# Clustered attention, soft MoE and a PReLU layer on one core: q's rounded part through PSUM, norm steps with a PSUM operand, a new order of attention's steps

## Chip, cores and metric

The kernel runs on one core of one Trainium2 chip. The metric is the device time of one execution in microseconds (us); lower is better. The time before is 498.64 us, the median of three runs (496.78 to 499.43).

## What is computed

Three layers follow one another. The attention has 2 x 8 = 16 heads of 768 tokens and 64 dimensions. Each token of q and k is assigned to one of 16 centroids of its head, and a query sees only keys of its own cluster:

```python
q_n = q / (np.linalg.norm(q, axis=-1, keepdims=True) + 1e-06)
k_n = k / (np.linalg.norm(k, axis=-1, keepdims=True) + 1e-06)
q_assign = np.argmax(np.einsum('bhsd,hcd->bhsc', q_n, c_n), axis=-1)
k_assign = np.argmax(np.einsum('bhsd,hcd->bhsc', k_n, c_n), axis=-1)
mask = q_assign[:, :, :, None] == k_assign[:, :, None, :]
scores = np.where(mask, scale * np.matmul(q, k.transpose(0, 1, 3, 2)), -1e9)
attn = np.exp(scores - np.max(scores, axis=-1, keepdims=True))
attn = attn / (np.sum(attn, axis=-1, keepdims=True) + 1e-09)
x = np.matmul(attn, v)
```

The result, 1536 tokens of 512, goes through a soft mixture of 8 experts (x @ phi, two softmaxes, w1, relu, w2), and then through x @ w_in, a PReLU with a slope per column, and @ w_out. All of it is float32.

## The kernel before

The 16 heads are worked on in 8 pairs. A head has six steps of 128 keys. In a step c of head h, `s2(h, c)` (L500) makes the scores of 128 keys against 768 queries in two halves of 384 columns: two matmuls for each half on TensorE (L514), and the exponential on ScalarE (L517) out of PSUM. `av` (L535) multiplies them by v (L542), and `acc` (L524) adds them up on GpSimd (L530). Some ten steps ahead, `s1` (L433) makes the scores of the later head once in lower precision (L448), so that VectorE can take each query's maximum (L455); `mrow` (L463) turns the maxima into a row (L484, L486) that `s2` uses as one more row of its operand. After a head, `sums` (L564) and `xnat` (L582) turn the sums and the output by TensorE (L571, L589); VectorE scales the output into x (L593, L597). After a pair, `xtr` (L604) turns x (L610), ScalarE copies it out (L614), and `logit` (L619) multiplies it by phi.

For float32 accuracy from TensorE's rounded float32 type, q and k are each split in a rounded part and the remainder. `put_high` (L418) rounds into the operands A and B (L420). `high` (L399) rounds a pair's whole q or k into a buffer `hi` in SBUF (L401), and `low` (L403) takes the remainder, in place: for q on VectorE, 768 columns at once (L407), for k on GpSimd, in two halves (L411). There is one `hi` for q and k together. `put_low` (L422) moves the parts to their lanes with four DMAs on SP's queue (L100).

For the assignment, `asg_norm` squares and sums q and k, `asg_root` (L274) takes the root by a start value and three Newton steps on VectorE, with its working values in a PSUM bank that it holds, and `asg_rn` (L304) adds 1e-6 and inverts it. The squared norms `n2` lie in SBUF (the tile `n` in the trace), so the first step (L285) and the addition (L307) read and write SBUF alone. The pairs are taken in six groups; the first two use ScalarE's root instead. `asg_sims`, `asg_nat` and `asg_pick` then find the nearest centroid.

`misc` (L127) gives the two PSUM banks for all such small work in turn. While a step holds one (`asg_nat` until the third `asg_pick`, `asg_root`, `win_bits`), all others get the other bank.

The order of the work is fixed when the kernel is built. Each call is entered by `add(key, function, ..., need=...)` with a place on a line that counts steps (L731 to L848), the places come from `TABLE` (L25), and the calls are made in the order of their places, put off until their needs are met (L860 to L873). Each engine, and SP's queue of DMAs, works through its own instructions in that order. Weights are loaded on SP's queue between them (`load_w`, L185): 16 units of 1 MB in attention, the other 16 after it (L194).

```python
    def high(p, nm):
        hi[p, nm] = t = ear.tile([P, S], F32R, name="hi")
        act.activation(t, raws[p][nm], AF.Copy)
```

Of the kernel before, what the change touches and what calls it, by code (L numbers as in the profile page):

```python
# [7 lines left out]
F32 = mybir.dt.float32  # L8
F32R = mybir.dt.float32r
# [23 lines left out]
    t_lo=-6.45, i_hk=-27.3, i_ph=-28.95, i_lk=-25.2, i_rt=-19.95, i_et=-18.5, z_lo=-8.6, md=(0, 1),  # L33
    ld=(0, -0.2, 0, 0, 0.2), e_sum0=7.85, e_sum1=11.3, e_xnat=10.3, lead=4, s1=-0.85, av=1.55,
    sum0=7.7, sum1=9.6, xnat=11.35, xtr0=11.7, xtr1=11.7, logit=12.5, t_sum0=7.15, t_sum1=14,
    t_xnat=13.9, t_xtr0=14.7, t_xtr1=15.4, t_logit=21.1, u_sum0=7.65, u_sum1=7.85, u_xnat=10.7,
    mr0=-1.35, mr1=1.15, mr2=2.85, z_mr0=-4.5, z_mr1=2.85, z_mr2=3.05, ph0=-8.35, ph1=-7.7,
    oh=-7.55, lo=-2.95, v=-4.6, raw=-25.1, sims=-14.75, nat=-13.85, p0=-13.5, p1=-14.35, p2=-12.05,
# [1 line left out]
    y_p0=-14.95, y_p1=-13.2, y_p2=-14.65, y_oht=-11.3, y_hq=-6.75, y_hk=-1.3, y_lq=-5.5, y_lk=-4.1,  # L40
    y_rn=-3, rest=-11.1, x0=5.5, x2=56.3, d0=-3.35, d1=2.2, d2=3.4, d3=-2.5, nl0=-14.45, nl1=-9.2,
    nl2=-4.8, nl3=-2.8, no0=-7.7, no1=-3.5, no2=-1.7, no3=-0.5, nr0=0.5, nr1=1.7, nr2=2.95, nr3=3.7,
    nrn=5.35, dz=(-2.7, 8.2), do0=1.6, do1=2.5, do2=2.8, do3=4.45, do4=3.3, sp=15, lke=0,
    w7=(4, 10), wc=(6, 3, 8), pipe=6, ws=13, wk=(0, 0, 3, 6, 3, 3, 3, 0, 6, 0, 6, 3),
# [2 lines left out]
    w=(
        ('r', -4.7, -1.7),
        ('r', 3.9, 6.5),
        ('r', 16.1, 16.1),  # L50
        ('r', 25.1, 30.1),
        ('r', 38.5, 38.5),
        ('r', 46.5, 54.5),
        ('r', 52.7, 53.3),
        ('r', 60.1, 62.1),
        ('r', 75.5, 75.5),
        ('r', 78.3, 79.3),
        ('r', 83.24, 84.24),
        ('a', 90.3, 92.3),
        ('a', 90.4, 92.4),  # L60
        ('r', 91.3, 93.7),
        ('b', 94.4, 96),
        ('c', 100.8, 101.8),
# [1250 lines left out]
```

## Time and profile before

| what | us |
|---|---|
| median of the three runs | 498.64 |
| the three runs | 499.43, 496.78, 498.64 |
| span of the profiled execution, first to last instruction | 495.9 |
| its own whole time | not listed apart from the three above |
| TensorE busy in the span | 451.4 (91%) |
| VectorE busy | 342.1 (69%) |
| ScalarE busy | 294.5 (59%) |
| GpSimd busy | 217.1 (44%) |
| TensorE's mean granted clock, of full speed | 0.986 |

Attention takes the first 290 us or so, the experts go to about 340 us, and the last layer takes the rest. In the names of the engines, PE is TensorE, PEld its loading of weights, DVE VectorE, ACT ScalarE, POOL GpSimd, and SP the queue that issues the DMAs. A busy share is a mean over stages with different limits, so a stretch is read by what its engines waited for. "Busy" also holds the time in which an instruction had been started and was held up.

### The profile page before, as it was taken

The page shows a single profiled execution, that of the slowest core. Times are in us where ns is not written, and L with a number is a line of the kernel's source. Part 1 is how long each engine was busy: PE and PEld are TensorE (multiplying, and loading weights), DVE is VectorE, ACT ScalarE, POOL GpSimd, SP SyncE. Part 2 cuts the span into 40 slices and gives each one's busy share as a digit, 9 for nine tenths or more (in the row PEclk, how much of TensorE's full clock was granted, in tenths as well). Part 3 has the DMA queues.
Part 4 walks back from the last instruction along what each step waited for, and adds up shares of the span by engine and source line. Part 5 has one row for each costly group of instructions (what it writes and reads, how often), then busy time and mean ns, then how long its engine had stood idle before and what let it go on. Part 6 is the DMA issues. An engine that isn't in the chain of part 4 may idle for free.

```text
span 495.9 us, 7750 instructions
## 1 busy us (share of the span) xinstructions
PE 451.4 (91%) x2694; PEld 299.7 (60%) x2694; DVE 342.1 (69%) x576; ACT 294.5 (59%) x538; POOL 217.1 (44%) x243
## 2 busy tenths in 40 slices
PE   3669899899999998989999899979899999999996
PEld 0336455565565655656565455436678888888885
DVE  3886989978999788798863442135799996544442
ACT  4846586585866868667665421126989885433431
POOL 5104777588777887677878200002443331000000
PEclk9997889999999999999999999999999999999999
DMA  8596555685676767544647489999322001200003
GB/s 283 150 299 189 156 145 185 149 266 170 163 200 185 195 222 212 154 131 123 230 138 256 192 325 351 388 397 398 102 85 86 0 0 49 79 1 0 1 1 127
DMA packets 32410, 84.10 MB, mean 170 GB/s; under 512 B 4402, under 2 KB 4742, under 8 KB 32372
## 3 DMA queue, kind: packets, MB, share of 16 engines
q1 hardware_dynamic: 32372, 83.62, 51.7%
q8 instruction: 21, 0.34, 0.3%
q14 instruction: 17, 0.14, 0.1%
HBM read 66.36 MB, written 3.19 MB: 140 GB/s over the span
## 4 chain that ended last, share of the span: by engine, by line
PE 54%; DVE 5%; issue 3%; ACT 3%; DMA 3%; POOL 1%; SPq 0%; ACTq 0%; POOLq 0%; DVEq 0%
PE ob L1206 8%; PE ob L1204 8%; PE ob L1205 8%; PE s L514 7%; PE ot L542 7%; PE s L448 3%; DMA unit_wr<-in_w 3%; PE s L995 2%; PE hp L1168 2%; PE L L1017 1%; PE misc L571 1%; DVE cs L455 1%; PE s L558 1%; POOL unit_wr L1101 1%; DVE unit_wr L407 1%
## 5 line engine op out<-in xcount | busy, mean ns | idle before, releaser
L530 POOL TENSOR_TENSOR ss<-ss,pt 128x384 f32<-128x384 f32 x150 | 147.0, 1020 | 40.8 <-PE ot L542 40.8
L455 DVE TENSOR_REDUCE cs<-s 128x1 f32<-128x768 f32 x91 | 86.2, 948 | 31.2 <-PE s L448 31.2
L517 ACT ACTIVATE pt<-s 128x384 f32<-128x384 f32 x160 | 70.0, 488 | 53.7 <-PE s L514 50.7
L514 PE MATMUL s<-A,B 97*128 97x384 f32 (+1 forms) x384 | 95.3, 370 | 2.2 <-ACT pt L517 2.1
L514 PEld LDWEIGHTS s<-A,B 97*128 97x128 f32 (+1 forms) x384 | 64.0, 195 | 27.5 <-issue 14.8
L1204 PE MATMUL ob<-unit_wr,gh 128*128 128x512 f32 x192 | 75.2, 392 | 0.5 <-ACT gh L1192 0.5
L1205 PE MATMUL ob<-unit_wr,gh 128*128 128x512 f32 x192 | 75.0, 390 | 0.2 <-POOL unit_wr L1101 0.2
L1206 PE MATMUL ob<-unit_wr,gl 128*128 128x512 f32 x192 | 75.1, 391 | 0.0
L1101 POOL TENSOR_TENSOR unit_wr<-unit_wr 128x256 fp32r<-128x256 f32 x32 | 26.0, 834 | 106.9 <-ACT unit_wr L1094 104.3
L448 PE MATMUL s<-B,A 96*128 96x384 f32 x192 | 57.4, 385 | 6.0 <-DVE cs L455 5.0
L542 PE MATMUL ot<-pt,raw_v 128*64 128x384 f32 x320 | 62.1, 501 | 0.0
L1190 DVE SCALAR_TENSOR_TENSOR g<-hp,sal,hs 128x768 f32<-128x768 f32 (+1 forms) x34 | 32.7, 967 | 26.1 <-ACT hs L1188 26.0
L448 PEld LDWEIGHTS s<-B,A 96*128 96x128 f32 x192 | 34.2, 202 | 21.6 <-DVE cs L455 16.7
L1188 ACT ACTIVATE hs<-hp,sgn 128x768 f32<-128x768 f32 (+1 forms) x34 | 29.1, 863 | 27.0 <-PE hp L1168 26.7
L1194 DVE TENSOR_TENSOR gl<-g,gh 128x768 fp32r<-128x768 f32 (+1 forms) x34 | 31.1, 915 | 15.1 <-ACT gh L1192 14.9
L1206 PEld LDWEIGHTS ob<-unit_wr,gl 128*128 128x128 f32 x192 | 36.0, 188 | 8.1 <-DVE gl L1194 0.3
L1205 PEld LDWEIGHTS ob<-unit_wr,gh 128*128 128x128 f32 x192 | 36.1, 188 | 7.5 <-POOL unit_wr L1101 1.1
L1204 PEld LDWEIGHTS ob<-unit_wr,gh 128*128 128x128 f32 x192 | 36.0, 188 | 7.0 <-ACT gh L1192 0.7
L1192 ACT ACTIVATE gh<-g 128x768 fp32r<-128x768 f32 (+1 forms) x34 | 27.4, 807 | 18.3 <-DVE g L1190 18.2
L542 PEld LDWEIGHTS ot<-pt,raw_v 128*64 128x64 f32 x320 | 20.3, 137 | 27.2 <-issue 26.4
L411 POOL TENSOR_TENSOR unit_wr<-unit_wr,hi 128x384 fp32r<-128x384 f32 x16 | 15.7, 1003 | 30.1 <-ACT n L281 14.4
L684 POOL TENSOR_TENSOR unit_wr<-unit_wr 128x256 uint32<-128x256 uint32 x26 | 19.2, 761 | 16.1 <-ACT ss L517 16.1
(184 smaller groups left out, 641.3 us busy)
## 6 DMA issues: line engine op xcount, KB each, us to landing
unit_wr<-in_w SPq DMA_DIRECT2D x16, 1024.0 KB
unit_wr<-in_w SPq DMA_DIRECT2D x18, 512.0 KB
unit_wr<-in_w_in SPq DMA_DIRECT2D x16, 512.0 KB
unit_wr<-in_w_out SPq DMA_DIRECT2D x7, 1024.0 KB
unit_wr<-in_qn SPq DMA_DIRECT2D x8, 384.0 KB
unit_wr<-in_kn SPq DMA_DIRECT2D x8, 384.0 KB
unit_wr<-in_qT SPq DMA_DIRECT2D x8, 384.0 KB
unit_wr<-in_kT SPq DMA_DIRECT2D x8, 384.0 KB
```

The costliest lines, as they stand in the source:

```text
L448: pe.matmul(ps[hf], a[:96, c * P:c * P + P], b[:96, hf * 384:hf * 384 + 384], start=True, stop=True,)
L455: dve.tensor_reduce(m, t, axis=AX.XY, op=ALU.max, negate=True)
L514: pe.matmul(ps[:, :384], b[:, c * P:c * P + P], a[:, hs], start=(i == 0), stop=(i == 1))
L517: act.activation(e[:, hs], ps[:, :384], AF.Exp, scale=0.125)
L530: (pool if h < T["sp"] else dve).tensor_tensor(ss[h][:, hs], ss[h][:, hs], sme[h, c][:, hs], op=ALU.add)
L542: pe.matmul(ot[h][hf * 64:hf * 64 + 64, :], v[:, c, par * 64:par * 64 + 64], e[:, hf * 384:hf * 384 + 384], start=(c == 0), stop=(c == 5),)
L1101: pool.tensor_tensor(wlo(i)[:, c], top[:, c], wh(i)[:, c].bitcast(F32), op=ALU.subtract)
L1190: dve.scalar_tensor_tensor(g, hv, sal[:, f:f + 1], hs, op0=ALU.mult, op1=ALU.max)
L1194: dve.tensor_tensor(gl, g, gh.bitcast(F32), op=ALU.subtract)
L1204: pe.matmul(ob[t], gh[:, c], wh(f), start=(f == 0), stop=False)
L1205: pe.matmul(ob[t], gh[:, c], wlo(f), start=False, stop=False)
L1206: pe.matmul(ob[t], gl[:, c], wh(f), start=False, stop=(f == 15))
```

## The change

Seven of the eight pairs (all but the first, which is made ahead of the attention) have q split in halves of 384 columns. ScalarE writes the rounded half into a `misc` bank of PSUM, and VectorE subtracts it from q into a buffer of its own, `lowq`. Each half's subtraction is entered right behind its rounding. k goes on through `hi`, and GpSimd takes its remainder. In the Newton root, the first step and the last write to PSUM or read from it, with one small copy added, and the addition of 1e-6 reads PSUM; for the first two groups (the root on ScalarE) it stays as it was. The places in `TABLE` are all set anew; two lines of them stand below for the many. A scratch space for DMAs that GpSimd would issue is cut to 1024.

```diff
-    oht=-9.55, hq=-6.05, hk=-1.95, lq=-7.3, lk=-5.1, y_v=-6.1, y_sims=-22.7, y_nat=-14.5,
+    nat=-13.65, p0=-13.5, p1=-13.7, p2=-11.45, oht=-9.65, hq0=-6.1, hq1=-3.7, hk=-4.55,
+    lq0=-8.9, lq1=-4.9, lk=-3.75, y_v=-8.7, y_sims=-23.9, y_nat=-18.15, y_p0=-20.3, y_p1=-14,
...
         if i == 0:
 
-            dve.tensor_scalar(x, x, 1e-30, None, op0=ALU.max)
             w = misc(hold=True)
...
-            nwt[g] = y, t
+            nwt[g] = y, t, z
+            dve.tensor_scalar(z, x, 1e-30, None, op0=ALU.max)
+            dve.tensor_copy(x, z)
             dve.tensor_scalar(
-                z.bitcast(U32), x.bitcast(U32), 1, None, op0=ALU.logical_shift_right
+                z.bitcast(U32), z.bitcast(U32), 1, None, op0=ALU.logical_shift_right
             )
...
         if i == 3:
-            dve.tensor_tensor(x, y, x, op=ALU.mult)
+            dve.tensor_tensor(z, y, x, op=ALU.mult)
+            dve.tensor_scalar(x, z, 1e-6, None, op0=ALU.add)
 
     def asg_rn(g):
         n = len(BATCH[g])
         x = n2[g][:, :n, :]
-        dve.tensor_scalar(x, x, 1e-6, None, op0=ALU.add)
+        if g < 2:
+            dve.tensor_scalar(x, x, 1e-6, None, op0=ALU.add)
...
-    hi = {}
-
-    def high(p, nm):
+    hi, lows = {}, {}
+
+    def high(p, nm, hf=None):
+        if hf is not None:
+            hi[p, nm, hf] = ps = misc(F32R)[:, :384]
+            act.activation(ps, raws[p][nm][:, hf * 384:hf * 384 + 384], AF.Copy)
+            return
...
-    def low(p, nm):
+    def low(p, nm, hf=None):
 
         t = raws[p][nm]
-        if nm == "qT" or T["lke"]:
+        if hf is not None:
+            if hf == 0:
+                lows[p] = cor.tile([P, S], F32R, name="lowq")
+            n = slice(hf * 384, hf * 384 + 384)
+            dve.tensor_tensor(
+                lows[p][:, n], t[:, n], hi.pop((p, nm, hf)).bitcast(F32), op=ALU.subtract
+            )
+            return
+        if nm == "qT":
             dve.tensor_tensor(t.bitcast(F32R), t, hi[p, nm].bitcast(F32), op=ALU.subtract)
             return
...
-        move(a2[:64, :], raws[h // 2]["qT"][lanes(h), :])
+        move(a2[:64, :], lows.get(h // 2, raws[h // 2]["qT"])[lanes(h), :])
...
-            add(s0 + T[z + "hq"] - LEAD, high, p, "qT", need=[("raw", p)], tag=("hq", p))
             add(s0 + T[z + "hk"] - LEAD, high, p, "kT", need=[("raw", p)], tag=("hk", p))
-            add(s0 + T[z + "lq"], low, p, "qT", need=[("hq", p), ("si", p), ("ph0", 2 * p), ("ph0", 2 * p + 1)], tag=("lq", p))
+            for i in range(2):
+                add(s0 + T[z + f"hq{i}"], high, p, "qT", i, need=[("raw", p)], tag=("hq", p, i))
+                add(s0 + T[z + f"lq{i}"], low, p, "qT", i, need=[("hq", p, i)] + ([("lq", p, 0)] if i else [("lo", 2 * p - 1)]), tag=("lq", p, i))
...
-    nc = bacc.Bacc("TRN2", target_bir_lowering=False, num_devices=1)
+    nc = bacc.Bacc(
+        "TRN2", target_bir_lowering=False, num_devices=1, dynamic_dma_scratch_size=1024
+    )
```

What the new places do is seen at the end of an odd head, here head 3, where pair 1 is finished and pair 3's q is split. VectorE's order there, before: `xnat` (L593, L597), the subtraction for q (L407), the maximum for the next head's last step (L455), and the picking of pair 4's centroids (L342, L344).

```order
L455 TENSOR_REDUCE cs<-s_1187 128x1
L593 TENSOR_TENSOR unit_wr<-misc_1197,rin 128x4x64
L597 TENSOR_TENSOR unit_wr<-misc_1197,rin 128x2x64
L407 TENSOR_TENSOR unit_wr<-unit_wr,hi 128x768
L455 TENSOR_REDUCE cs<-s_1229 128x1
L342 TENSOR_TENSOR misc_1233<-misc_1233,rn 128x384
L344 TENSOR_REDUCE unit_wr<-misc_1233 128x24
```

And the same place now (L610 and L614 are `xnat`, L472 the maximum, L419 a half's subtraction, L347 to L353 the picking, L592 and L595 `sums`):

```order
L610 TENSOR_TENSOR unit_wr<-misc_1196,rin 128x4x64
L614 TENSOR_TENSOR unit_wr<-misc_1196,rin 128x2x64
L472 TENSOR_REDUCE cs<-s_1202 128x1
L419 TENSOR_TENSOR lowq<-unit_wr,misc_1224 128x384
L472 TENSOR_REDUCE cs<-s_1238 128x1
L347 TENSOR_TENSOR misc_1244<-misc_1244,rn 128x384
L349 TENSOR_REDUCE unit_wr<-misc_1244 128x24
L352 TENSOR_TENSOR misc_1244<-misc_1244,unit_wr 128x384
L353 TENSOR_TENSOR misc_1244<-misc_1244,iotab 128x384
L472 TENSOR_REDUCE cs<-s_1278 128x1
```

`xnat` has moved ahead of one maximum, and the subtraction of 768 columns out of SBUF has become one of 384 with PSUM as its second operand; the other half follows some steps later.

TensorE's order at that place, before: the maxima's scores of head 4's fifth step (L448), the similarities of pair 4 (L322), `xnat` (L589), and at once `xtr` (L610), which reads what VectorE makes of `xnat`.

```order
L448 MATMUL s_1187<-B_0_124,A_0_121 128x384 x2
L322 MATMUL misc_1191<-unit_wr,CB 32x384 x4
L589 MATMUL misc_1197<-cs,osb 128x128 x3
L610 MATMUL misc_1205<-cs,unit_wr 128x128 x3
L610 MATMUL misc_1211<-cs,unit_wr 128x128 x3
L514 MATMUL s_1218<-A_2_123,B_2_126 128x384
```

Now, with L606 for `xnat`, L465 for the maxima's scores, L327 for the similarities and L627 for `xtr`:

```order
L606 MATMUL misc_1196<-cs,osb 128x128 x3
L465 MATMUL s_1202<-B_0_124,A_0_121 128x384 x2
L327 MATMUL misc_1206<-unit_wr,CB 32x384 x4
L627 MATMUL misc_1212<-cs,unit_wr 128x128 x3
L627 MATMUL misc_1218<-cs,unit_wr 128x128 x3
L531 MATMUL s_1229<-A_2_123,B_2_126 128x384
```

The scores and the similarities now lie between `xnat` and `xtr`.

ScalarE's order at that place, before: the copies of `xtr` (L614), the exponentials of head 3's first step (L517), k's rounding into `hi` (L401), and k's rounding into B (L420).

```order
L614 COPY osb<-misc_1205 128x384
L614 COPY osb<-misc_1211 128x384
L517 ACTIVATE ss<-s_1218 128x384
L517 ACTIVATE ss<-s_1222 128x384
L401 ACTIVATE hi<-unit_wr 128x768
L420 ACTIVATE B_1_125<-unit_wr 64x768
```

Now (L631 are the copies, L407 q's rounded half, L534 the exponentials, L437 k's rounding into B):

```order
L631 COPY osb<-misc_1212 128x384
L631 COPY osb<-misc_1218 128x384
L407 ACTIVATE misc_1224<-unit_wr 128x384
L534 ACTIVATE ss<-s_1229 128x384
L534 ACTIVATE ss<-s_1233 128x384
L437 ACTIVATE B_1_125<-unit_wr 64x768
```

q's rounded half stands ahead of the exponentials, and k's rounding into `hi`, which before stood between them and B, has gone to an earlier place.

## Rows read from the trace of the kernel before

**Rows 1.** Windows by stage: attention's middle, and the experts' loads (columns in the first line).

```profile
core 0: us, PE busy (x) PEld busy (x) DVE busy (x) ACT busy (x) POOL busy (x), PEclk, DMA share, GB/s
48.00:264.00 216.00, 202.94 (x1147) 124.54 (x1146) 183.57 (x316) 149.55 (x302) 166.06 (x176) 0.98 0.61 178
290.00:340.00 50.00, 46.30 (x531) 22.89 (x530) 12.04 (x38) 10.43 (x24) 0.00 (x0) 1.00 1.00 384
```

**Rows 2.** Waits, 48 to 264 us: who waited for whom, total us, times, longest.

```profile
POOL unit_wr L411 <- ACT B L420: 12.7, 6, 3.2
ACT hi L401 <- DVE unit_wr L407: 7.7, 6, 2.1
PE misc L610 <- DVE unit_wr L593: 4.7, 6, 1.1
PE misc L484 <- DVE cs L455: 4.0, 6, 2.1
PE s L448 <- DVE cs L455: 1.3, 4, 0.7
PE misc L571 <- ACT ohm L486: 1.2, 1, 1.2
```

**Rows 3.** Groups by line, 48 to 264 us: shapes and count, busy us, mean ns, idle before.

```profile
L517 ACT ACTIVATE pt<-s 128x384 f32<-128x384 f32 x136 | 59.3, 488 | 42.7 <-PE s L514 39.8 <-POOL ss L530 2.3
L407 DVE TENSOR_TENSOR unit_wr<-unit_wr,hi 128x768 fp32r<-128x768 f32 x7 | 12.5, 1786 | 0.6 <-ACT A L420 0.6
L401 ACT ACTIVATE hi<-unit_wr 128x768 fp32r<-128x768 f32 x13 | 11.0, 843 | 7.7 <-DVE unit_wr L407 7.7
L307 DVE TENSOR_SCALAR n<-n 128x24 f32<-128x24 f32 (+1 forms) x4 | 10.2, 2548 | 0.0
L342 DVE TENSOR_TENSOR misc<-misc,rn 128x384 f32<-128x384 f32 x6 | 3.3, 552 | 0.0
L285 DVE TENSOR_SCALAR n<-n 128x48 f32<-128x48 f32 (+1 forms) x3 | 2.7, 911 | 0.0
L300 DVE SCALAR_TENSOR_TENSOR misc<-unit_wr,misc 128x48 f32<-128x48 f32 (+1 forms) x10 | 2.0, 202 | 0.3
```

**Rows 4.** Timeline, 118 to 125 us: start, us, engine, line, and idle before.

```profile
118.74 3.89 POOL L530 TENSOR_TENSOR ss<-ss,pt 128x384 f32<-128x384 f32 x4
119.01 0.42 DVE L593 TENSOR_TENSOR unit_wr<-misc,rin 128x256 f32<-128x256 f32 x1 [0.30 <-PE misc L589]
...
119.58 0.85 PE L610 MATMUL misc<-cs,unit_wr 128*128 128x128 f32 x6 [0.61 <-DVE unit_wr L593]
119.94 3.51 DVE L407 TENSOR_TENSOR unit_wr<-unit_wr,hi 128x768 fp32r<-128x768 f32 x1 [0.31 <-ACT A L420]
...
124.37 0.30 PE L484 MATMUL misc<-cs 128*70 128x128 f32 x1 [0.34 <-DVE cs L455]
```

**Rows 5.** Timeline, 53 to 59 us.

```profile
53.23 3.77 DVE L307 TENSOR_SCALAR n<-n 128x24 f32<-128x24 f32 x1
...
55.00 1.97 POOL L530 TENSOR_TENSOR ss<-ss,pt 128x384 f32<-128x384 f32 x2
...
58.21 0.30 PE L484 MATMUL misc<-cs 128*70 128x128 f32 x1 [2.14 <-DVE cs L455]
```

**Rows 6.** Windows of 2 us, 60 to 66 us (columns as in the first group).

```profile
60.00:62.00 2.00, 1.76 (x6) 1.14 (x4) 1.93 (x4) 1.22 (x3) 1.93 (x2) 0.50 0.90 190
62.00:64.00 2.00, 1.92 (x7) 0.97 (x8) 1.93 (x6) 1.91 (x5) 0.00 (x0) 0.50 0.96 202
64.00:66.00 2.00, 2.00 (x9) 0.41 (x5) 2.00 (x3) 0.47 (x1) 1.18 (x2) 0.50 0.60 201
```

**Rows 7.** Timeline, 187 to 189 us.

```profile
188.04 0.27 ACT L486 ACTIVATE ohm<-misc 6x128 fp32r<-6x128 f32 x1
...
188.45 0.53 PE L571 MATMUL misc<-cs,ss 128*128 128x128 f32 x3 [1.21 <-ACT ohm L486]
```

**Rows 8.** Timeline of SP's queue at the end of attention: start, us, what it issued.

```profile
297.20 26.12 SPq L194 DMA_DIRECT2D unit_wr<-in_w  x13
```

More of the change, by code (lines that the diff above doesn't have):

```diff
@@ L32 @@
     """,
[L33 to L38, printed above, removed]
@@ L39 @@
-    oht=-9.55, hq=-6.05, hk=-1.95, lq=-7.3, lk=-5.1, y_v=-6.1, y_sims=-22.7, y_nat=-14.5,
[L40 to L44, printed above, removed]
@@ L45 @@
-    dl=(-55, -33.4, 0.5, 6.5, 13.9, 20.1, 23.5, 31.9, 37.7, 44.6, 49.9, 54.7, 61.9, 68.1, 71.7,
-        77.5),
-    w=(
[L48 to L63, printed above, removed]
+    t_lo=-6.8, i_hk=-29.85, i_ph=-25.75, i_lk=-27.7, i_rt=-17.65, i_et=-19.8, z_lo=-12.1,
@@ new lines @@
+    md=(0, 1), ld=(-0.4, -0.25, 0, -0.05, 0.2), e_sum0=7.65, e_sum1=10.8, e_xnat=10.3, lead=4,
+    s1=-0.85, av=1.55, sum0=7.7, sum1=9.7, xnat=11.15, xtr0=11.35, xtr1=11.8, logit=12.45,
+    t_sum0=5.55, t_sum1=18.8, t_xnat=12.45, t_xtr0=14.05, t_xtr1=14.15, t_logit=20.6,
+    u_sum0=6.8, u_sum1=8.15, u_xnat=10.5, mr0=-1.25, mr1=1.2, mr2=2.85, z_mr0=-3.8, z_mr1=2.25,
+    z_mr2=3.75, ph0=-9.75, ph1=-8, oh=-7.65, lo=-1.35, v=-3.5, raw=-23.4, sims=-14.75,
+    nat=-13.65, p0=-13.5, p1=-13.7, p2=-11.45, oht=-9.65, hq0=-6.1, hq1=-3.7, hk=-4.55,
@@ new lines @@
+    lq0=-8.9, lq1=-4.9, lk=-3.75, y_v=-8.7, y_sims=-23.9, y_nat=-18.15, y_p0=-20.3, y_p1=-14,
+    y_p2=-17.95, y_oht=-12.4, y_hq0=-5.65, y_hq1=-4.15, y_hk=-1.2, y_lq0=-8.2, y_lq1=-9.2,
+    y_lk=-5.3, y_rn=-13.45, rest=-9.95, x0=6.45, x2=52, d0=-2.95, d1=2.4, d2=3.4, d3=-0.45,
+    nl0=-12.85, nl1=-9.35, nl2=-5, nl3=-1.75, no0=-9.5, no1=-3.5, no2=-2.2, no3=-0.2, nr0=1.05,
+    nr1=-0.25, nr2=1.75, nr3=2.8, nrn=5.05, dz=(-2.9, 7.95), do0=1.5, do1=2.5, do2=2.75,
+    do3=4.75, do4=1.65, sp=15, w7=(4, 10), wc=(6, 3, 8), pipe=6, ws=13,
@@ new lines @@
+    wk=(0, 0, 3, 6, 3, 3, 3, 0, 6, 0, 6, 3),
+    dl=(-55.4, -36.6, 1.15, 2.55, 12.6, 20.5, 26.15, 31.9, 37.85, 44.5, 46.5, 54.9, 61.05, 67.5,
+        72.4, 78.1),
+    w=(
+        ('r', -2.65, -2.65),
+        ('r', 6.65, 8),
+        ('r', 18.4, 22.35),
+        ('r', 24.8, 31.4),
+        ('r', 38.3, 38.3),
+        ('r', 46.6, 53.8),
+        ('r', 52, 55.4),
+        ('r', 58.95, 67.95),
+        ('r', 79.6, 84),
+        ('r', 80.95, 81.45),
+        ('r', 86.74, 87.44),
+        ('a', 89.3, 90),
+        ('b', 91.3, 94.5),
+        ('a', 91.8, 92.45),
+        ('r', 93.75, 97.8),
+        ('c', 99, 102.3),
@@ L296, in asg_root @@
             return
-        y, t = nwt[g]
+        y, t, z = nwt[g]
         dve.tensor_tensor(t, y, x, op=ALU.mult)
@@ L760, in clustered_attention_soft_moe_prelu_ffn @@
             add(s0 + T["oh"] - LEAD, put_oh, h, need=[("oht", p), ("s2", h - 3, 5)], tag=("oh", h))
-        add(s0 + T[z + "lo"], put_low, h, need=[("lq", p), ("lk", p), ("s2", h - 2, 5), ("ph0", h), ("ph1", h)], tag=("lo", h))
+        add(s0 + T[z + "lo"], put_low, h, need=[("lq", p, 0), ("lq", p, 1), ("lk", p), ("s2", h - 2, 5), ("ph0", h), ("ph1", h)], tag=("lo", h))
     def exp_table():
@@ L779, in clustered_attention_soft_moe_prelu_ffn @@
     add(T["i_et"], exp_table, need=["i_rt"], tag="et")
-    done.update([("ph0", 1), ("oht", 0), ("p2", 0), ("hq", 0), ("hk", 0), ("ph0", 0), ("ph1", 0), ("oh", 0), ("lq", 0), ("root", 1, 3), ("raw", 1), ("raw", 0)])
+    done.update([("ph0", 1), ("oht", 0), ("p2", 0), ("hq", 0), ("hk", 0), ("ph0", 0), ("ph1", 0), ("oh", 0), ("lq", 0, 0), ("lq", 0, 1), ("root", 1, 3), ("raw", 1), ("raw", 0)])
     done.update(("s2", h, 5) for h in range(-3, 0))
```

2 lines of the change are left out of this document (1 added, 1 removed).

## The prediction

> **What bounds the kernel now.** I began with the windows by stage. From 48 to 264 us, most of the attention, TensorE is busy 202.9 of 216 us at a mean granted clock of 0.98 of full speed [rows 1]: it is the engine that sets the pace, and about 13 us of this stretch are its idle time, which is all that a change of waits can win there. From 290 to 340 us the DMA engines' share is 1.00 [rows 1]: the experts' weights set the pace. These stages answer to different causes, so I look for the effect of this change in the first.
>
> Next come the waits of that stretch. Of TensorE's 13 us, 4.7 us stand before `xtr` (L610), behind VectorE's `xnat` (L593); 4.0 us before `mrow` (L484), behind VectorE's maxima (L455); 1.3 us before `s1` (L448), behind the same; 1.2 us before `sums` (L571), behind ScalarE [rows 2]. So what TensorE waits for is nearly always VectorE being late.
>
> Then the groups by line say why it is late. A step on 24 columns (L307) takes 2548 ns on average and L285 takes 911, where a like step that works with a PSUM operand (L300) takes 202; the subtraction of q (L407) takes 1786 ns for 768 columns [rows 3]. The timeline shows what these steps do in that time. GpSimd's four additions that began at 118.74 us ended at 122.63; VectorE's L407, begun at 119.94, ended at 123.45, 0.82 us later [rows 4]. GpSimd's additions ended at 56.97, and L307 at 57.00 [rows 5]. The stalled step ends when a run of GpSimd's steps does. In the first case TensorE's L484 waited 0.34 us for what was queued behind it on VectorE, in the second 2.14 us [rows 4, 5].
>
> **The rule and the row.** The row shows a wait that lasts through several additions of GpSimd, about one us each [rows 4]. The Trainium skill ("SBUF — State Buffer", section "Who interferes with whom") says that VectorE's steps with two SBUF inputs, or in a two-port mode, share a port pair with GpSimd, and that whoever issues first holds it for one whole instruction. By that, a stall would be one addition at most. That changes the sum, and it is a rival below; I take the rows.
>
> **The change, part by part.**
>
> *VectorE's steps.* Out go seven L407, four L307 and three L285, 12.5 + 10.2 + 2.7 = 25.4 us of this stretch [rows 3]. In come 14 halves with a PSUM operand. The nearest row is L342, also 384 columns and in PSUM, at 552 ns: 7.7 us. The norm steps become three small ones for each of four groups, at L300's 0.20 us: 2.4 us [rows 3]. VectorE is freed of 25.4 - 10.1 = 15.3 us. Only what TensorE waits for counts, though: of its 4.0 us before L484 I take 3.5 as gone (lower bound 0, upper 4.0). What is late next there is the picking in VectorE's queue, which stays as it is; for it I leave 0.5. The 1.3 us before L448 I leave as they are.
>
> *TensorE's clock.* Between 60 and 66 us the granted clock is 0.50, the lower of the two levels (1.2 GHz for 2.4) [rows 6], just after the longest of these waits, the 2.14 us that ended at 58.21 [rows 5]. TensorE was busy 5.7 us of these 6, and would need 2.8 us less at full clock. But VectorE was busy 5.9 of the same 6 [rows 6] and would hold it. Without that wait I expect no drop there, and take 1.5 us (0 to 2.8).
>
> *The order of `xnat` and `xtr`.* The order shows two matmul groups, one of `s1` and the similarities, between them where there was nothing. In the example TensorE waits 0.61 us between L589 and L610 for VectorE's 0.42 us and what lies around them [rows 4]. The work put between is longer than that, so the 4.7 us should go; the six waits are in six pairs [rows 2], and the last two pairs, after 264 us, keep `xtr` right behind `xnat`. VectorE has one more maximum to take now between `xnat` and the subtraction, so I take 4.2 (0 to 4.7).
>
> *ScalarE.* Seven whole roundings at 843 ns go, 5.9 us. 14 halves come. What a half into PSUM takes no row shows; half of the 843 is one bound, L517's 488 ns for 384 columns out of PSUM the other [rows 3]. I take 488, the nearer in shape: 6.8 us, so 0.9 us more on an engine busy 149.6 of 216 us [rows 1]. I cost it at nothing; the exponentials behind it cover it, and if they came late L514 would wait. ScalarE's own 7.7 us of waiting for L407 (q and k shared one `hi`) goes [rows 2]. One wait that follows from such a queue, L571's 1.2 us behind L486 [rows 7], goes as well, because k's rounding has left the place ahead of it: 1.2 (0 to 1.2).
>
> *GpSimd.* The subtraction of k moves to a place where its `hi` has long been there, so its 12.7 us of waiting for ScalarE's B goes [rows 2]. GpSimd is busy 166 of 216 us [rows 1] and TensorE never waits for it in the rows of waits, so: nothing.
>
> *SP's queue.* The DMAs are as many as before. `put_low` and its four transfers come some 1.6 steps later, behind one transfer of the maxima's row and ahead of the other; both are ready ahead of the next head by several steps. The weights' loads of attention's last two heads are in another order; after attention 13 loads go out at 297.20 us in one row [rows 8], once x has been read, and they move with attention's end. Nothing for either, with 2 us on each side kept for the range, also for the start-up before 48 us, whose order is new too. The smaller scratch space I cost at nothing: these transfers are SP's.
>
> *The new wait.* Each subtraction stands right behind its rounding, so VectorE now waits for ScalarE 14 times, and behind VectorE stand the maxima for which TensorE waits. At worst each costs TensorE a half's whole 0.49 us [rows 3], 6.9 in all; at best nothing, since ScalarE's halves are entered behind work already done. TensorE has v's matmuls between; I take 2.0.
>
> The sum: 3.5 + 1.5 + 4.2 + 1.2 - 2.0 = 8.4 us. The span of 495.9 us becomes 487.5. Only the span of the profiled execution is known; the median of the three runs is 2.74 above it, and I carry this over: 490.2 us.
>
> **The rivals.**
>
> *A new wait gives most of it back.* VectorE, now tied to ScalarE twice a pair, is late again. If seven of the 14 waits cost as much as the one known wait behind ScalarE's queue, 1.2 us [rows 7], 8.4 us go instead of 2.0: a gain of 2.0, 496.6 us. For it: VectorE is still the engine waited for. Against it: it has 15 us less to do.
>
> *VectorE sets the pace, not TensorE.* Then all its 15.3 us come off: 483.3 us. Against it, TensorE's 202.9 of 216 [rows 1], which would then have to run with no gap.
>
> *The stall is one addition long, and the rest is something that stays* (the skill's rule, as a mechanism here: only some 1.0 us of each stalled step goes). Then 1.1 of the 2.14 us before L484 stays, and with it perhaps the clock's 1.5: 492.8 us. Against it: both stalls end with GpSimd's run [rows 4, 5].
>
> *Nothing is won.* TensorE's gaps come back elsewhere, since each end of a head has several steps that feed each other: 498.6 us.
>
> *Slower: the one bank.* From `asg_nat` to the third `asg_pick` one PSUM bank is held, and the second half of q now goes through the other in that time, between two uses by `sums`. ScalarE then waits for VectorE's reading of `sums`, with its exponentials behind it, VectorE for ScalarE, and TensorE for both. At 1.2 us [rows 7] for each of 14 halves that is 16.8 us, against the 10.4 that the rest gains: 505.0 us. It decides from 0.74 us a half on. Against it: in the new order the reading of `sums` stands a whole maximum ahead of the half.
>
> **How the numbers follow.** About 0.5%, 2.5 us, is what a measurement of this kernel can tell from no change. So faster means below 496.1 us, slower above 501.1.
>
> - The forecast, 486 to 494 us: 0.60, all faster.
> - Mostly given back, 493 to 499: 0.17, of it 0.09 faster, 0.07 the same, 0.01 slower.
> - VectorE sets the pace, 483.3: 0.07, faster.
> - One addition long, 492.8: 0.05, faster.
> - Nothing won, 498.6: 0.05, the same.
> - The one bank, 505.0: 0.06, slower.
>
> Faster 0.81, the same 0.12, slower 0.07. Low end: all upper bounds together (4.0 + 2.8 + 4.7 + 1.2, and no new wait) are 12.7 us, 485.9; with 2 us for start and end, 484. High end: 498, which takes in most of the second case and leaves out the slower one. That leaves out about 0.15.
>
> **What would show it.** Right: no step of VectorE on 24 or 48 columns over 0.5 us after 48 us; the 14 halves at some 0.55 us each; the waits of L484's and L610's successors at 0.5 us or less in all; no stretch at half clock near 60 us; TensorE idle some 5 us between 48 us and the end of the same work. Wrong: VectorE's halves with long idle time behind ScalarE; the successor of L514 waiting for exponentials; a drop of the clock in another place; or attention ending 8 us earlier with the last expert's load landing where it does now.

## The result and the profile after

The changed kernel takes 492.76 us (median of 20 runs, 491.11 to 497.57). The kernel before, run beside it on the same chip, takes 497.57 us (20 runs, 493.89 to 499.87). The ratio is 0.9918, with a 95% interval from 0.9894 to 0.9941: 4.1 us less, between 2.9 and 5.3. The forecast was 490.2 us within 484 to 498, from a median of 498.64. So the direction and the range held, and the gain is about half of the forecast one. A ratio in this document leaves out executions that took over 1.5% more than the fastest one of their kernel. The profiled execution took 491.77 us with a span of 489.6; before, the span was 495.9.

The windows by stage, with the three at 60 to 66 us between them (columns as in [rows 1]):

```profile
48.00:264.00 216.00, 206.55 (x1190) 127.49 (x1186) 171.78 (x331) 156.13 (x319) 170.19 (x182) 1.00 0.62 181
60.00:62.00 2.00, 1.57 (x8) 0.90 (x6) 1.97 (x4) 0.87 (x2) 1.95 (x3) 1.00 0.79 281
62.00:64.00 2.00, 2.00 (x12) 0.88 (x11) 1.32 (x4) 1.65 (x4) 2.00 (x4) 1.00 0.13 51
64.00:66.00 2.00, 0.96 (x6) 0.56 (x4) 1.86 (x4) 2.00 (x5) 2.00 (x3) 1.00 0.67 146
290.00:340.00 50.00, 46.69 (x631) 24.51 (x623) 15.61 (x42) 13.87 (x31) 2.96 (x4) 1.00 1.01 387
```

Against [rows 1] TensorE's idle time from 48 to 264 us falls from 13.1 to 9.5 us, with VectorE busy 11.8 us less. The stretch at half clock [rows 6] is gone. The experts' stage stays at a DMA share of 1.0, as forecast.

The waits from 48 to 264 us (waiter, who is waited for: us in total, times, longest):

```profile
DVE lowq L419 <- ACT misc L407: 9.3, 7, 1.8
PE s L465 <- DVE cs L472: 3.2, 7, 0.6
PE misc L588 <- DVE oh L359: 2.4, 2, 1.6
PE misc L501 <- DVE cs L472: 1.5, 2, 0.9
PE misc L627 <- DVE unit_wr L610: 0.2, 1, 0.2
```

These answer to [rows 2]. `xtr` (L610 before, L627 now) goes from 4.7 to 0.2 us. `mrow` (L484, now L501) goes from 4.0 to 1.5 us. `s1` (L448, now L465) goes up from 1.3 to 3.2 us, and a wait of `sums` (L588) for the picking's last step, 2.4 us, is new. VectorE does wait for ScalarE's halves, 9.3 us in seven times; what TensorE pays for that is at most the rise of L465.

The groups by line (shapes and count, busy us, mean ns, idle before):

```profile
L419 DVE TENSOR_TENSOR lowq<-unit_wr,misc 128x384 fp32r<-128x384 f32 x14 | 7.7, 550 | 9.3 <-ACT misc L407 9.3
L407 ACT ACTIVATE misc<-unit_wr 128x384 fp32r<-128x384 f32 x14 | 6.9, 495 | 2.2 <-PE s L465 1.5 <-DVE rin L595 0.2
L306 DVE TENSOR_SCALAR n<-misc 128x24 f32<-128x24 f32 x2 | 0.4, 182 | 0.1
L291 DVE TENSOR_SCALAR misc<-n 128x48 f32<-128x48 f32 x2 | 0.4, 200 | 0.0
```

The durations forecast from [rows 3] held: 550 ns for a half's subtraction (552 taken), 495 for its rounding (488 taken), 180 to 220 for the norm steps (202 taken). No stall is left in them.

**The start-up lost 3 us.** In the kernel before, TensorE's and VectorE's timeline at 20 to 25 us, and ScalarE's first exponential (start, us, engine, line, and idle before), read:

```profile
22.53 1.01 PE L448 MATMUL s<-B,A 96*128 96x384 f32 x2 [0.41 <-DVE cs L455]
23.32 0.45 DVE L307 TENSOR_SCALAR n<-n 128x24 f32<-128x24 f32 x1
23.70 0.90 PE L333 MATMUL misc<-cs,unit_wr 128*128 128x128 f32 x3 [0.16 <-ACT unit_wr L327]
38.50 1.13 ACT L517 ACTIVATE ss<-s 128x384 f32<-128x384 f32 x2 [1.52 <-PE s L514]
```

and in the changed kernel:

```profile
21.84 0.88 DVE L312 TENSOR_SCALAR n<-n 128x24 f32<-128x24 f32 x1 [3.49 <-ACT n L283]
23.74 0.90 PE L338 MATMUL misc<-cs,unit_wr 128*128 128x128 f32 x3 [3.67 <-ACT unit_wr L332]
41.56 1.13 ACT L534 ACTIVATE ss<-s 128x384 f32<-128x384 f32 x2 [2.42 <-PE s L531]
```

Pair 1's inverse norms (L307, now L312) and its turned similarities (L333, now L338) are now entered ahead of the next scores, and both engines stand still for them, 3.49 and 3.67 us. The first exponential comes 3.06 us later.

The last step of attention, TensorE's last `logit`, in the kernel before and in the changed one:

```profile
291.50 1.21 PE L627 MATMUL L<-osb,phit 128*32 128x384 f32 x8
```

```profile
285.83 1.21 PE L644 MATMUL L<-osb,phit 128*32 128x384 f32 x8
```

From the first exponential to here it is 253.0 us before and 244.3 after, 8.7 us less, where the sum said 8.4 for the whole span. From here to the end of the span it is 204.4 and 203.8. So the middle gave about as much as was forecast, and the start took 3.1 of it back. The windows between the two marks, before and after, hold the same 1340 matmuls:

```profile
38.50:292.71 254.21, 238.17 (x1340) 144.76 (x1340) 199.85 (x359) 168.40 (x342) 179.21 (x190) 0.98 0.62 185
```

```profile
41.56:287.04 245.48, 233.22 (x1340) 142.70 (x1340) 186.25 (x370) 170.36 (x349) 177.50 (x190) 1.00 0.64 193
```

TensorE's idle time falls from 16.04 to 12.26 us, by 3.8. Its busy time, for the same work, falls by 4.95. More than half of the 8.7 is thus time at half clock that is gone.

One part of that was not in the sum. Windows of the kernel before, then of the changed one, from 38.5 to 42 us (columns as above); the first had been at half clock from 36 us on:

```profile
38.50:42.00 3.50, 3.50 (x15) 1.76 (x15) 1.64 (x5) 2.40 (x5) 1.40 (x2) 0.50 1.03 287
```

```profile
38.50:42.00 3.50, 2.12 (x6) 1.78 (x6) 3.47 (x7) 1.08 (x2) 0.00 (x0) 1.00 0.93 332
```

Before, TensorE is busy throughout 38.5 to 42 us at the lower clock level, 1.2 GHz; at full clock that work would take 1.75 us less. In the changed kernel's profile no stretch in which TensorE works is at half clock.

### The profile page after: what moved, and what is told of

Read it like the earlier page. It is cut to its first block, busy times and chain, and to the rows that moved or that the text cites. A ratio compares the mean times of both kernels' runs of the same rounds, so it can differ in the third digit from the quotient of the medians.

```text
span 489.6 us, 7783 instructions
## 1 busy us (share of the span) xinstructions
PE 447.1 (91%) x2694; PEld 298.3 (61%) x2694; DVE 329.1 (67%) x587; ACT 296.5 (61%) x545; POOL 215.4 (44%) x243
## 4 chain that ended last, share of the span: by engine, by line
PE 69%; DVE 12%; ACT 7%; DMA 6%; issue 3%; SPq 1%; POOL 1%; ACTq 0%; DVEq 0%; POOLq 0%
PE s L531 11%; PE ot L559 10%; PE ob L1224 8%; PE ob L1222 8%; PE ob L1223 8%; PE s L465 6%; DVE cs L472 4%; DMA unit_wr<-in_w 4%; PE hp L1186 2%; PE s L1013 2%; PE misc L588 2%; DMA unit_wr<-in_w_in 2%; PE L L1035 2%; PE misc L327 1%; ACT pt L534 1%
## 5 line engine op out<-in xcount | busy, mean ns | idle before, releaser
L534 ACT ACTIVATE pt<-s 128x384 f32<-128x384 f32 x160 | 69.8, 489 | 49.2 <-PE s L531 48.5
L472 DVE TENSOR_REDUCE cs<-s 128x1 f32<-128x768 f32 x91 | 86.3, 949 | 16.8 <-PE s L465 16.1
L531 PE MATMUL s<-A,B 97*128 97x384 f32 (+1 forms) x384 | 93.6, 365 | 2.5 <-ACT pt L534 2.4
L465 PE MATMUL s<-B,A 96*128 96x384 f32 x192 | 58.0, 390 | 7.3 <-DVE cs L472 6.5
L465 PEld LDWEIGHTS s<-B,A 96*128 96x128 f32 x192 | 34.3, 205 | 21.3 <-DVE cs L472 18.0
L592 DVE TENSOR_REDUCE misc<-misc 128x3 f32<-128x384 f32 x32 | 17.9, 558 | 11.7 <-PE misc L588 7.5
```

The source lines that it names most:

```text
L465: pe.matmul(ps[hf], a[:96, c * P:c * P + P], b[:96, hf * 384:hf * 384 + 384], start=True, stop=True,)
L472: dve.tensor_reduce(m, t, axis=AX.XY, op=ALU.max, negate=True)
L531: pe.matmul(ps[:, :384], b[:, c * P:c * P + P], a[:, hs], start=(i == 0), stop=(i == 1))
L534: act.activation(e[:, hs], ps[:, :384], AF.Exp, scale=0.125)
```

## The experiments

Two things could bring the gain: the steps on VectorE that no longer stall (q's halves, the norm steps), or the order of calls. The first eight runs take one part of the change away, or make one part alone.

**The norm steps undone** (the rest of the change stays):

```diff
+            dve.tensor_scalar(x, x, 1e-30, None, op0=ALU.max)
-            dve.tensor_scalar(z, x, 1e-30, None, op0=ALU.max)
-            dve.tensor_copy(x, z)
...
-        if g < 2:
-            dve.tensor_scalar(x, x, 1e-6, None, op0=ALU.add)
+        dve.tensor_scalar(x, x, 1e-6, None, op0=ALU.add)
```

> The changed kernel with the norm steps of before (first step and the addition of 1e-6 on SBUF alone), all else as changed. Stall theory: the four additions take 1 to 4 us again, TensorE waits for the maxima behind them, 2 to 4.5 us more than the changed kernel's 492.8: 495 to 497.3. Order theory (all the gain is the order's): 492.8 within 1 us, since the slow steps lie beside other work. By the rule that a stall is one addition of GpSimd long (1.0 us), no such step would take more than 1.2 us and the time would rise by 1 us at most.

Measured: 493.51 us, ratio to before 0.9946 (0.9904 to 0.9988). The 12 runs fall in two groups, seven of 491.2 to 493.9 and five of 496 to 501.3. The profiled one is the longest, and its timeline (GpSimd, VectorE, TensorE) shows what it lost:

```profile
142.43 8.71 POOL L544 TENSOR_TENSOR ss<-ss,pt 128x384 f32<-128x384 f32 x9
147.24 5.30 DVE L309 TENSOR_SCALAR n<-n 128x48 f32<-128x48 f32 x1
151.09 1.41 POOL L698 TENSOR_TENSOR unit_wr<-unit_wr 128x256 uint32<-128x256 uint32 x2
153.66 1.51 PE L624 MATMUL misc<-cs,unit_wr 128*128 128x128 f32 x6 [4.96 <-DVE unit_wr L611]
```

One step on 48 columns lasts 5.30 us and ends at 152.54, where GpSimd's run of eleven steps ends (152.50). Behind it stands `xnat`'s scaling, and TensorE waits 4.96 us; from 152 to 158 us its clock is at half. In the new order the norm steps are worth little in most executions, and some 9 us in this one, in which a stalled step meets a long run of GpSimd. Over all 12, the three longest included, the mean is 495.2 us, 2.3 above the changed kernel's 492.9. The other four of the upper group have no trace, so their cause is not shown. The order alone, below, has two such groups as well (eight executions of 497.7 to 500.5 us, four of 503.1 to 507.2), and its traced execution, one of the longest, has the same stall (5.29 us, from 148.54 on) and a wait of TensorE of 5.0 us behind it.

**q's rounded halves in SBUF:**

```diff
-            hi[p, nm, hf] = ps = misc(F32R)[:, :384]
+            hi[p, nm, hf] = ps = ear.tile([P, 384], F32R, name="hiq", bufs=2)
```

> The changed kernel with q's rounded halves in two SBUF buffers of 384 columns instead of PSUM banks, all else as changed, order included. Stall theory: the 14 subtractions have two SBUF operands again and some take 1.5 to 4 us instead of 0.55; time up by 2 to 5 us, 495 to 498. Order theory: no change, 492.8 within 1 us. Bank theory (the halves in PSUM delay others by holding a bank): down by 1 to 2 us, 491.

Measured: 501.18 us, ratio 1.0102 (1.0058 to 1.0146). The group of the halves, and TensorE's two waits for the maxima, 48 to 264 us:

```profile
L419 DVE TENSOR_TENSOR lowq<-unit_wr,hiq 128x384 fp32r<-128x384 f32 x14 | 16.5, 1175 | 8.9 <-ACT hiq L407 8.8
```

```profile
PE s L465 <- DVE cs L472: 8.4, 14, 1.5
PE misc L501 <- DVE cs L472: 3.0, 6, 0.9
```

A half that works out of SBUF alone takes 1175 ns rather than 550, and the waits for the maxima grow by 5.2 and 1.5 us. With PSUM as the operand 8.4 us are won, all in the new order. That is more than the 2 to 5 us expected of it.

**The new order alone** (both edits above together):

> The new order, with norm steps on SBUF as before and q's halves in SBUF: the order alone, without PSUM operands. Stall theory: the gain of the order at xnat and xtr stays (4 us), the start-up's loss stays (3 us), the stalls are back: 496 to 499, near the time before. Order theory: 492.8, as the change.

Measured: 499.22 us, ratio 1.0074 (1.0037 to 1.0111). Without its PSUM operands the new order is slower than the kernel before. By the runs with the old start-up, below, 2 to 3 us of that are the start-up's.

**`xtr` right behind `xnat` again** (places as before the change):

```diff
-    xnat=11.15, xtr0=11.35, xtr1=11.8,
+    xnat=11.35, xtr0=11.7, xtr1=11.7,
```

> The changed kernel with xnat put back right ahead of xtr in seven pairs (three numbers of the table). My sum: TensorE waits 0.6 to 1.1 us before xtr six times again, 4 us more: 496 to 497.5. Rival (VectorE's stalls made those waits, or the waits move elsewhere): 492.8 to 494.

Measured: 497.24 us, ratio 1.0025 (0.9986 to 1.0065), 4.5 us above the changed kernel. The wait is back, and the halves wait longer too (12.8 us rather than 9.3):

```profile
PE misc L627 <- DVE unit_wr L610: 5.8, 6, 2.2
DVE lowq L419 <- ACT misc L407: 12.8, 9, 1.9
```

The time fits this part of the sum, 4.2 us, but the trace shows that the waits before `xtr` are not all of it: between the first exponential and the last `logit` TensorE idles 2.9 us longer than in the changed kernel (15.2 and 12.3) and is busy 2.2 us longer, with a drop of the clock at 246 us, and the first exponential comes 1.0 us later (42.57).

**The start-up's order as before** (four places):

```diff
-    z_lo=-12.1, y_nat=-18.15, y_p0=-20.3, y_rn=-13.45,
+    z_lo=-8.6, y_nat=-14.5, y_p0=-14.95, y_rn=-3,
```

> The changed kernel with four places of the start-up as before: the second pair's addition and inversion of the norms, its transposes and its first picking stand behind the first head's maxima again instead of ahead of them. Start-up theory (the first exponential came 3.1 us later because VectorE's and TensorE's queues wait 3.5 us for ScalarE's root): first exponential near 38.5 us instead of 41.6, time 489 to 490.5, faster than both kernels. Rival (the later start is set by the DMAs or by the order of the weights' loads): 492 to 493.

Measured: 489.69 us, ratio 0.9880 (0.9832 to 0.9927). A second time, beside other kernels:

> The changed kernel with the start-up's order as before, a second time, beside the kernel above. 489.7 us (488 to 491.5), some 3 us less than the changed kernel; if the first result was one chip's or one day's, 492 to 493.

Measured: 490.43 us, ratio 0.9869 (0.9836 to 0.9903). This beats both kernels, by 2 to 3 us and by 6 to 7. The first exponential comes at 39.79 us in the first trace and at 38.93 in the second, back near where it was before the change (38.50; 41.56 in the changed kernel):

```profile
38.93 1.13 ACT L534 ACTIVATE ss<-s 128x384 f32<-128x384 f32 x2 [2.42 <-PE s L531]
```

So the start-up's order is what the change gave away: 1.8 and 2.6 us of the 3.06 come back.

**The norm steps alone, in the kernel before:**

> The kernel before with the norm steps through PSUM and nothing else. Stall theory: the waits of 2.1 us at 56 us and 0.7 at 219 go, and with the first the clock's drop: 2 to 4.5 us faster, 493 to 495.5. If the stalled steps only lay beside other work: 497 to 498.

Measured: 493.93 us, ratio 0.9961 (0.9935 to 0.9987), some 2 us. From 48 to 264 us the granted clock is 1.00, so the drop of [rows 6] is gone with the 2.14 us wait of [rows 5]. Three waits of TensorE, before `mrow` (L487), `s1` (L451) and `s2` (L517), and the group of q's subtraction (L407 before, L410 here):

```profile
PE misc L487 <- DVE cs L458: 1.1, 4, 0.4
PE s L451 <- DVE cs L458: 2.4, 5, 0.7
PE s L517 <- ACT pt L520: 1.3, 1, 1.3
```

```profile
L410 DVE TENSOR_TENSOR unit_wr<-unit_wr,hi 128x768 fp32r<-128x768 f32 x7 | 20.6, 2938 | 0.6 <-ACT A L423 0.6
```

The wait before `mrow` falls from 4.0 to 1.1 us, although q's subtraction, which nothing in its code changes, is now stalled 8.1 us longer in all than in [rows 3]. That extra stall is not free, though. The wait before `s1` rises from 1.3 to 2.4 us, and the one before `s2`, 0.2 before, is 1.3. It comes by way of ScalarE, which waits for the stalled subtraction (L410) before it rounds k (L404), and is then late with an exponential (L520, at 58.36 us):

```profile
55.11 2.34 DVE L410 TENSOR_TENSOR unit_wr<-unit_wr,hi 128x768 fp32r<-128x768 f32 x1
57.49 0.84 ACT L404 ACTIVATE hi<-unit_wr 128x768 fp32r<-128x768 f32 x1 [0.69 <-DVE unit_wr L410]
```

Between the first exponential and the last `logit` TensorE idles 15.55 us, 0.5 less than before, and is busy 236.06, 2.1 less: the gain in this trace is nearly all the clock's. Stalled time of VectorE is not itself a price; the waits behind it are, also those that pass through another engine.

**q's halves alone, at the old places** (the code of the halves as in the change, the norm steps as before):

```diff
-    hq=-6.05, lq=-7.3, y_hq=-6.75, y_lq=-5.5,
+    hq0=-7.3, hq1=-7.3, lq0=-7.3, lq1=-7.3, y_hq0=-5.5, y_hq1=-5.5, y_lq0=-5.5, y_lq1=-5.5,
```

> The kernel before with q's halves through PSUM at the old place of the subtraction, norm steps as before. Stall theory: waits of 0.3 us in each of three or four pairs go: 0.5 to 2 us faster, 495.6 to 497. New-wait theory: slower by 1 to 3 us, since two roundings of ScalarE now stand ahead of VectorE's maximum.

Measured: 505.51 us, ratio 1.0167 (1.0102 to 1.0231). The halves themselves are as short as in the changed kernel, 548 ns. The waits, 48 to 264 us:

```profile
ACT misc L402 <- DVE lowq L414: 4.8, 3, 2.1
PE misc L322 <- DVE unit_wr L689: 4.3, 2, 2.4
ACT misc L402 <- DVE unit_wr L689: 4.0, 2, 2.5
```

ScalarE's halves (L402) and TensorE's similarities (L322) wait for VectorE to have read the PSUM bank that they get, in `low` (L414) and in `win_bits` (L689). That is the slower rival of the prediction, in the order in which it was not forecast. The time lies above both expectations. The trace is of the shortest of six executions (499.54 us; four took 505.4 to 506.2).

**Both steps, at the old places:**

> The order of before, with both new kinds of steps: norm steps through PSUM and q's halves through PSUM into a buffer of their own, each half's rounding and subtraction at the old place of the subtraction. Stall theory: 3.5 to 5 us under the 497.6 of before, with the clock's drop near 60 us gone in most executions: 492.5 to 494. Order theory: 497 to 498. New-wait theory: VectorE waits for ScalarE ahead of each half, and the time is 498 or more.

Measured: 504.39 us, ratio 1.0170 (1.0118 to 1.0222), with the same waits for the bank. In this trace TensorE idles 18.7 us between the first exponential and the last `logit`, 2.6 more than before, and is busy 244.1, 5.9 more, with the clock down in four places. So most of the loss reaches the time through the clock.

Neither explanation holds by itself: the steps alone are 8 us slower than the kernel before, and the order alone 3.7, of which 2 to 3 are the start-up's. The PSUM halves need places at which a bank is free, and in the new order the maxima wait for halves that are longer. The norm steps show no gain in the new order while q's halves lie in SBUF (1.0102 beside 1.0074, with intervals that overlap). The smaller scratch space for DMAs is in every run that has q in halves and in no other. It was not tried alone; in the traces before and after, all DMAs that the kernel issues are SP's. The ratios to the kernel before in one table (its last row has q in halves where it is not in PSUM, the first has it whole):

| order | neither step | norm steps | q through PSUM | both |
|---|---|---|---|---|
| before's | 1 | 0.9961 | 1.0167 | 1.0170 |
| the change's | 1.0074 | 1.0102 | 0.9946 | 0.9918 |

**How long is a stall?** The kernel before, with GpSimd's additions in quarters:

```diff
-        for n0 in range(0, S, 384):
-            hs = slice(n0, n0 + 384)
+        for n0 in range(0, S, 192):
+            hs = slice(n0, n0 + 192)
```

> The kernel before, with each of GpSimd's additions of 384 columns made as two of 192, so that one instruction is about half as long and a run of them as long as before or a little longer. Theory (a stalled step of VectorE waits until the whole run of GpSimd's steps ends): the steps on 24 and 48 columns (L309 in this kernel's numbers or near it, 2548 ns on average before) and the subtraction of 768 columns (1786 ns before) keep their mean durations within some 20%, so above 2000 ns and above 1450 ns, and the longest still end with GpSimd's last step. Rival (the stall is one GpSimd instruction long, as the Trainium skill's page SBUF — State Buffer, section Who interferes with whom, has it): the stalled part halves, so some 1300 ns for the small steps and some 1300 ns for the subtraction. The time of the whole kernel is not what this run is for: 495 to 510 us, since GpSimd has twice as many instructions.

Measured: 514.06 us, one run. Groups from 48 to 264 us, and the timeline of the case of [rows 5]:

```profile
L530 POOL TENSOR_TENSOR ss<-ss,pt 128x192 f32<-128x192 f32 x252 | 141.3, 608 | 29.6 <-PE ot L542 29.6
L407 DVE TENSOR_TENSOR unit_wr<-unit_wr,hi 128x768 fp32r<-128x768 f32 x7 | 14.5, 2067 | 0.6 <-ACT A L420 0.6
L307 DVE TENSOR_SCALAR n<-n 128x24 f32<-128x24 f32 x2 | 9.7, 4854 | 0.0
L307 DVE TENSOR_SCALAR n<-n 128x48 f32<-128x48 f32 x2 | 6.9, 3466 | 0.0
```

```profile
52.79 2.27 POOL L530 TENSOR_TENSOR ss<-ss,pt 128x192 f32<-128x192 f32 x4
53.51 5.15 DVE L307 TENSOR_SCALAR n<-n 128x24 f32<-128x24 f32 x1
55.00 1.44 POOL L684 TENSOR_TENSOR unit_wr<-unit_wr 128x256 uint32<-128x256 uint32 x2
56.38 2.25 POOL L530 TENSOR_TENSOR ss<-ss,pt 128x192 f32<-128x192 f32 x4
```

GpSimd's instruction is 40% shorter (608 ns, 1020 before) and the stalls are longer: 2067 ns for q's subtraction (1786 before), 5.15 us for the step that took 3.77. L307 lasts through the last nine of ten GpSimd instructions and ends at 58.66, with the last of them (58.63). In such cases the stall goes with the length of GpSimd's run, not of its instruction. The theory's 20% held for the subtraction (16% longer) and not for the small steps: the four L307 take 4.2 us on average, 2.5 before. The runs are longer too, as two quarters take 1216 ns where one addition took 1021, and the time lies 4 us above what was expected.

**The picking ahead of `sums`.** The new wait of L588, 2.4 us, looked like the next thing to win. On top of the start-up's old order:

```diff
-    p2=-11.45,
+    p2=-12.35,
```

> The changed kernel with the start-up's order as before (measured at 489.69 us) and the third step of the picking entered ahead of sums in attention's middle, so that the PSUM bank that the picking holds is free before sums and q's second half ask for banks. Theory (the wait of 1.6 and 0.8 us before sums in the changed kernel is the one bank's doing, and TensorE's idle time is what counts): both waits go and up to 2.4 us are won, 487.5 us; a little less where the maxima behind the picking come 1.1 us later. Rival (VectorE is as late as before, only in another place): 489.7 us, with the maxima's waits longer by what the bank's wait loses, or 491 if the delay of 1.1 us comes in each of six pairs at a place without slack.

Measured: 507.71 us, ratio 1.0201 (1.0153 to 1.0248), 17 us worse than without it. Both expectations missed. The wait became

```profile
PE misc L588 <- DVE oh L359: 11.7, 5, 2.9
```

When the picking's hold on its bank ends in the order of calls, the next step that asks gets just that bank, and TensorE waits until VectorE, with one more maximum ahead of it, has read it. This wait grew by 9.3 us; with three of its five times the clock falls (0.50 from 60 to 66 us, 0.69 from 98 to 102, 0.58 from 162 to 166). Between the first exponential and the last `logit` TensorE idles 10.7 us longer than in the second trace without the edit (22.1 and 11.4) and is busy 4.0 us longer for the same matmuls. That is 14.7 of the 15.3 us between the two spans.

**The picking behind `sums`,** so that `sums` gets the other bank:

```diff
-    p2=-11.45,
+    p2=-10.3,
```

> The changed kernel with the start-up's order as before (490.43 us in the last call) and the third step of the picking entered behind the second sums of a head's end rather than ahead of it. Theory, mended after the run with the picking ahead of sums: when the picking's hold on its bank ends in the order of calls, the next step that asks gets that very bank, whose last reader, the picking's last step on VectorE, is still to come; behind sums, the hold is still on, sums gets the other bank, and the waits of 1.6 and 0.8 us before sums go. Then 2.4 us are won: 488.0 us, and no wait before sums for the picking at all. Rival (the wait moves on to the step that now comes next on that bank, the turning of the picked one-hot rows, or the maxima come late behind the later picking): 490 to 492 us, with waits of that step or before the row of maxima over 1 us.

Measured: 497.17 us, ratio 1.0071 (1.0035 to 1.0108). The wait of `sums` is gone, as the mended theory has it, but the rival's wait takes its place, at the turning of the picked rows (L382):

```profile
PE misc L382 <- DVE oh L359: 7.0, 6, 1.3
```

That is 4.6 us more than the 2.4 removed. The time missed both expectations. The median is 6.7 us above that without the edit, which ran on another chip; the ratios, each to the kernel before on its own chip, differ by 2.0%, some 10 us. The two traced spans are 6.3 us apart, of which 5.8 are idle time of TensorE between the first exponential and the last `logit`. The picking stands at a place where an earlier and a later one are both worse.

## Why the prediction was right in direction and twice too large

*The start-up's order.* This is the step that failed outright: "Nothing for either, with 2 us on each side kept for the range, also for the start-up before 48 us, whose order is new too." The start-up cost 3.06 us in the trace, and undoing its order wins 2 to 3 us in the runs. The places in the table and the order of instructions at 20 us were there to be read: pair 1's inverse norms ahead of the first maxima, behind ScalarE's root. The prediction looked at three places in attention's middle, and at none in the start-up.

*The order of `xnat` and `xtr`.* 4.2 forecast, 4.5 in the waits, 4.5 in the run that undoes it. Right, though part of that run's 4.5 is the clock's and the start's.

*The waits before L484.* 3.5 forecast. Of 4.0 us 1.5 are left as the wait for the maxima and 0.3 as one for a half, so 2.2 went. The stalls are gone, as said; what stays is VectorE's other work.

*TensorE's clock.* 1.5 forecast for 60 to 66 us. The drop is gone, which is worth at most 2.8 us [rows 6], and another drop, at 36 to 42 us, went as well, worth at most 1.75. The second one was not in the sum. For the same matmuls TensorE's busy time fell by 4.95 us. The clock also differs from execution to execution: of 55 executions of the kernel before, beside the experiments on one chip, the 15 with a mean granted clock of 0.998 or more took 493.9 us on average and the other 40 497.5, while nine of the changed kernel's 20 had such a clock and took 492.1, and the other eleven 493.7. That points to the clock as a large part of the gain, but the clock and the waits come together, and no run parts them.

*L571's wait.* 1.2 of gain forecast. It went, and the wait of 2.4 us for the picking's bank came in the same step of the work: a loss of 1.2.

*The new wait.* 2.0 forecast. VectorE waits 9.3 us for the halves; TensorE's waits for the maxima before L465 rose by 1.9. Right in size, but that the halves cause it is not shown: with `xtr` right behind `xnat` the halves wait 12.8 us, and L465 only 1.3.

Together, the parts read from the traces are 2.2 + 4.5 + 2.8 + 1.75 - 1.2 - 1.9 = 8.2 us, with the clock's two at their upper bounds, against 8.7 measured between the two marks and 8.4 forecast. That the middle's sum came out so near is luck: the waits were to give 6.9 us and TensorE's idle time fell by 3.8, while the clock was to give 1.5 and TensorE's busy time fell by 4.95. L484 and L571 gave less than was taken, and the clock more. Of the measured 8.7 the start takes 3.1 and the end adds 0.6: 6.2 us, and the two spans differ by 6.3. That is more than the 4.8 between the medians and the 4.1 of the ratio. The profiled execution of before is a longer one of its kind: its span and the 2.17 us that lie outside it after the change would make 498.1, where the median is 497.57. The change's profiled run is 1 us below its own median. So the 2.74 us that the forecast carried over from span to median were some 0.6 too many.

*The signs and the range.* The short steps and halves came as named, and so did the clock near 60 us. TensorE was to idle some 5 us, and idles 9.5; the waits of L484's and L610's successors were to be 0.5 us in all, and are 2.0. A sign of being wrong came as well, VectorE's halves with 9.3 us of idle time behind ScalarE. And the range left out more than the 0.15 that it names: its own list puts 0.07, 0.05 and 0.06 outside of it, 0.18 before the edges of the second case.

*The rivals.* "VectorE sets the pace" did not come: TensorE still idles 9.5 us while VectorE has 44. "The stall is one addition long" was stated with the Trainium skill's rule ("SBUF — State Buffer", section "Who interferes with whom": whoever issues first holds the shared port for one whole instruction). The quarters speak against it in this kernel: instructions 40% shorter, stalls longer. The prediction's own reading, that a stalled step ends when GpSimd's run does, is too wide as well: it holds for both cases that it shows, and not for all (see the last section). "The one bank" came in the old order, at 504 to 506 us where it said 505.0; that the number fits is luck. The argument against it, that in the new order the reading of `sums` stands a whole maximum ahead of the half, fits what the two orders show. Its count of 14 waits of 1.2 us was not how it came: five waits of ScalarE, 8.8 us, TensorE's own for the same bank, and the clock.

## What to carry to other kernels

A change to a table of places moves the whole program: compare the order at every stage in which an engine idles, the start-up too, before a term is put at nothing. Price a stalled engine by the waits behind it on the engine that sets the pace, not by its busy time, and follow them through the other engines: 8 us more of stall brought some 2 us of other waits here, and one stall of 5.3 us a wait of 5. Part the time between two marks into busy and idle time of that engine: the clock hides in the first. A cheaper step that needs a scarce PSUM bank pays only with an order in which the bank has been read by the time it is asked for; try the step and the order apart and together, as each alone can lose.
